# Keys and queries turned on VectorE, and a group's cells sorted by array shape, in an mLSTM and SwiGLU kernel

## The chip, the cores and the metric

The kernel runs on one core of a Trainium2 chip. The metric is the device time of one execution in microseconds. The core has a matrix engine (TensorE, in the profile PE for matmuls and PEld for weight loads), a vector engine (VectorE, DVE), a scalar engine (ScalarE, ACT), a general engine (GpSimd, POOL) and a queue engine (SyncE, SP) that issues all transfers here. Matmuls read SBUF and write PSUM[...]; VectorE and ScalarE read the results from there.

## The reference

Two blocks follow one another. The first is an mLSTM cell over 4 batches, 8 heads, 768 steps, head size 40; the second is a SwiGLU feed-forward over the 3072 tokens of width 320, with an inner width of 1536. All is float32.

```python
def _attn_ref(q, k, v, i_gate, f_gate, o_gate):          # B, H, S, D = 4, 8, 768, 40
    for t in range(S):
        kt, vt, qt = (k[:, :, t], v[:, :, t], q[:, :, t])
        m_new = np.maximum(f_gate[:, :, t] + m, i_gate[:, :, t])
        f_stab = np.exp(f_gate[:, :, t] + m - m_new)
        i_stab = np.exp(i_gate[:, :, t] - m_new)
        m = m_new
        C = f_stab[:, :, None, None] * C + i_stab[:, :, None, None] * np.einsum('bhd,bhe->bhde', vt, kt)
        n = f_stab[:, :, None] * n + i_stab[:, :, None] * kt
        h_tilde = np.einsum('bhde,bhe->bhd', C, qt)
        nq = np.einsum('bhd,bhd->bh', n, qt)[:, :, None]
        denom = np.maximum(np.abs(nq), 1.0)
        o = 1.0 / (1.0 + np.exp(-o_gate[:, :, t]))
        y[:, :, t] = o * h_tilde / denom

def _moe_ref(x, w_gate, w_val, w_out):                   # x: (3072, 320), from y
    g = x @ w_gate
    silu = g * (1.0 / (1.0 + np.exp(-g)))
    val = x @ w_val
    return silu * val @ w_out
```

## The kernel before

The sequence is cut into cells of 128 steps: 6 cells per batch, 24 in all, each with its 8 heads. Three cells form a group, so there are 8 groups, two per batch. Inside a cell the recurrence is written as attention: scores of k against q, weighted by the gates, times v. What came before the cell is carried as a state `C` (with the normaliser as one column more), which is multiplied with q (`qT`, after its product with the decay `e`) and renewed by the product of k with the weighted v (`add`). A group's 384 tokens then go through the feed-forward: 12 hidden blocks and a projection of 36 matmuls.

Each step is a Python generator. A string says in which order the generators are advanced; with that it sets the order on every engine[...]. In `GROUP`, a letter with a number names one step: `H` a hidden block, `J` a third of one 128-token projection, `k` loads of k and q, `v`, `o`, `e`, `w` other loads, `T` the turning of k and q so that the head size lies on the partitions, `S` the scores, `A` the products with v, with the carried state and the renewal of the state, `F` the finishing of a cell (it divides, gates and turns its output), `W` the weights from the gates. While group g is in the feed-forward, the cells of group g+1 are computed and those of g+2 are loaded.

```python
GROUP = """
H0*3 o0*2 e0*2 H1*3 S0*4 G0*2 H2*3 k0*4 v0 H3*3 o1*2 e1*2 H4*3 S1*4 G1*2 H5*3 k1*4 v1 H6*3 o2*2 e2*2 H7*3 S2*4 G2*2
H8*3 k2*4 v2 H9*3 H10*3 w0 w1 H11*3 A0*5 F0*6 w2 J0 T0*4 W0 J1 A1*5 F1*6 W1 J2*3 T1*4 W0*2 J3 A2*5 F2*6 W0 W2 J4 T2*4 W1*2
J5*3 W2*2 W1 J6 W2 J7 J8*3
"""
# START: a longer string for the first two groups, with the gates and the loading of the weights (cut)

    def load_kq(u):
        un = get(u)
        for a, name in ((k, "k"), (q, "q")):
            for two in range(2):
                dst = un[name].rearrange("p (j two) d -> p two j d", two=2)
                nc.sync.dma_start(out=dst[:, two, :, 0:D], in_=tokens(a, u)[:, two * PR:(two + 1) * PR, :])
                yield

    def turn(u, tag):                        # PR = 4 pairs of heads, L = 128
        un = units[u]
        for name, n in (("k", GC), ("q", 2 * GC - 1)):
            tp = psum.tile([128, PR, L], F32, name="tp_kq", tag=tag, bufs=2)
            for j in range(PR):
                nc.tensor.transpose(tp[:, j, :], un[name][:, 2 * j:2 * j + 2, :].rearrange("p h d -> p (h d)"), ident)
            yield
            un[name + "T"] = work.tile([128, PR, L], F32, name=name + "T", bufs=n)
            nc.scalar.copy(un[name + "T"], tp)
            yield

    def attend(u):
        ...
        ys = un["ys"] = [psum.tile([128, PR // 2, L], F32, name="yT", tag="gen") for _ in range(2)]
        ...
        if c > 0:                            # carried state times q: array shape 64*64
            for j in range(PR):
                for two in range(2):
                    r = slice(two * DP, two * DP + DP)
                    onto(two * PR + j, old[r, j, :], un["qT"][r, j, :], False)
            yield
        if c + 1 < NB:                       # renewal of the state: 128*64
            add = psum.tile([128, PR, D1], F32, name="add", tag="cell", bufs=NCELL)
            for h in range(H):
                two, j = divmod(h, PR)
                nc.tensor.matmul(add[two * DP:(two + 1) * DP, j], lhsT=un["k"][:, 2 * j + two, :],
                                 rhs=un["v_w"][:, h, :], start=(j == 0), stop=(j == PR - 1), skip_group_check=True)
            yield
            new = C_ring[u % 2]
            if c > 0:
                d = dec[:, c - 1, b * PR:(b + 1) * PR].unsqueeze(2).to_broadcast([128, PR, D1])
                kept = work.tile([128, PR, D1], F32, name="kept", bufs=1)
                nc.gpsimd.tensor_tensor(kept, old[:, :, 0:D1], d, op=ALU.mult)
                yield
                nc.vector.tensor_tensor(new[:, :, 0:D1], add, kept, op=ALU.add)
            ...
        for h in range(H):                   # weighted scores times v: 128*64
            onto(h, un["v"][:, h, :], un["w"][:, h, :], True)
        yield

    def hidden(g, m, i0=0, i1=GC):
        ...
        ps = [psum.tile([128, TW], F32, name="gv_ps", tag="gen") for _ in range(2)]      # 4 banks in "gen"
        for kc in range(NKC):
            for i in range(2):               # two halves of 64 rows: 64*128
                r = slice(i * HP, (i + 1) * HP)
                nc.tensor.matmul(ps[i][:, cols], lhsT=wgv_sb[r, kc, ts(m, 128)], rhs=xts[g][r, kc, cols], ...)
        yield
        sg = gsp.tile([128, TW], F32, name="sg")
        nc.scalar.activation(sg[:, cols], ps[0][:, cols], AF.Sigmoid if g else AF.Silu)
        yield
        if g:
            nc.vector.tensor_tensor(sg[:, cols], sg[:, cols], ps[0][:, cols], op=ALU.mult)
        nc.vector.tensor_tensor(h_ring[:, (g * NFC + m) % NH, cols], sg[:, cols], ps[1][:, cols], op=ALU.mult)
        yield

    def project(g, i, part):                 # 128*128
        if part == 0:
            hs[g, i] = psum.tile([128, DM], F32, name="o_ps", tag="gen")
        ...                                  # 4 of its 12 matmuls per part; a copy and a store after the last
```

Of the kernel before, what the change touches and what calls it, by code (L numbers as in the profile page):

```python
# [9 lines left out]
F32 = mybir.dt.float32  # L10
# [13 lines left out]
H0*3 o0*2 e0*2 H1*3 S0*4 G0*2 H2*3 k0*4 v0 H3*3 o1*2 e1*2 H4*3 S1*4 G1*2 H5*3 k1*4 v1 H6*3 o2*2 e2*2 H7*3 S2*4 G2*2  # L24
H8*3 k2*4 v2 H9*3 H10*3 w0 w1 H11*3 A0*5 F0*6 w2 J0 T0*4 W0 J1 A1*5 F1*6 W1 J2*3 T1*4 W0*2 J3 A2*5 F2*6 W0 W2 J4 T2*4 W1*2
J5*3 W2*2 W1 J6 W2 J7 J8*3
# [3 lines left out]
pad0 kq1*2 pad0 bar1 v1 pad1 bar2 kq1 pad2 pad4 kq1 pad4 pad5 pad2 which kq0*2 runA v2 pad1 kq0 o2 T1 pad5 T1 tgA  # L30
decA kq0 M1 decA v0 tgA M1 pad3*2 kq2 runB kq2 T1 T0 kq2 W1 M2 T0 T1 o1 W1 M2 kq2 decB o2 decA S1 B decB W1 decB
bar0 W2 B S1 M0 S1 W0 T0 B*2 T0 M0 W0 o0 S0 o0 o1 R0 W0 W2 S0 R0 W2 G2 S0 decA*2 T2 R0 T2*2 G2 T2 R0 E1 S1 S2 C0 R1
R2 R3 C0 G0 R2 S2 G0 R1 G1 S2 C0 R1 C4 R1 A0 C1 store G1 A0*2 F0 v3 A1 R9*2 A1*2 R9 F0 E2 R9 kq3 S2 kq3*2 C1 F0*2
kq3 F0 R2 C1 R2 R8 A1*2 F1 store tgB store H0 kq5 F1 kq5 T3 H0 kq5 tgB A2 kq5 A2 C4 T3 kq8 F1*2 T3 w3 H0 e3 F1 A2
T3 e3 C4 C3 w7 A2*2 C3 e4 decB R3 T5 R3 C2*2 C3 R3 C13 decB H2 C2 R6 F2 C8 R4 H1 R6 W3 F2 H2 T5 H1 S3 R6 W3 R6 H1
H2 R4*2 C13 R4 F2*2 kq4*2 C13 F2 C5 kq4 H3 kq4 C8 R8 W7 R8 W3 C8 C5 H5 o5 H3 o5 W3 R5 S3 C5 C9 R5 H3 R5 T4 C9 R5 H4
H5 T4 R10 H5 o3 C6 o3 C9 C6 H4 R10*2 H6 G5 R8 C6 H4 S3 kq7*2 C7 w4 G5 C7 w5 H9 kq8 S3 G3 v7 H6 G3 v4 C7 o4 R10 H6
C11 e5 T4 C11 H9 A3 T4 A3*2 W4 kq8 H9 H7 C12*2 W4 C11 kq8 W5 A3 R13 C12 A3 R7 W4 S4 H7 F3 R7 W4 H12 R7*2 C14 R11 H7
S4 R14 C14 R11 W5 T5 C14 S4 R11 H8 H12 R16 F3 e5 e4 H12 C17 R11 v6 C17 H13 H8 F3 C10 H8 R12 W5 C17 C10 v5 o4 H11
C10 C18 R15 C18 w6 H13 S4 kq7 v8 T7 C15 C18 H13 H10 w8 C15 H11 T5 C15 H11 C16 R17 C16 R19 A4 H10 T7 kq7 H10 A4*2 F3  # L40
C16 A4*2 C20 F4 S5 kq6 C19 H14 S5 W6 kq6 W7 S5 kq6 S5 C19 kq6 H14 A5*2 C19 C20 W8 J3 W7 H14 R18 C20 F3 J6 C21 F5 W7
W8 C21 W8 J0 C21 F5 C23 J7 G4 C23 J1 W8 C22 C23 C22 W6 J4 F5 C22 J8 W6 G4 F4 F5 J2 F5 J8*2 F4*2 J5 W6 F4 J2*2 J5
T7*2 T8 J5 T8*3 T6*4
# [19 lines left out]
def kernel(  # L63
# [50 lines left out]
    NCONV, NCELL = 2, 2  # L114
    GATED = range(100)
# [37 lines left out]
# [3 lines that stand above are left out]
            for two in range(2):  # L156
                dst = un[name].rearrange("p (j two) d -> p two j d", two=2)
                nc.sync.dma_start(out=dst[:, two, :, 0:D], in_=tokens(a, u)[:, two * PR:(two + 1) * PR, :])  # L158
                yield
# [133 lines left out]
    def pads(r):  # L293
        if r < NRQ:
            nc.vector.memset(q_ring[r][:, :, D:], 0.0)
        nc.vector.memset(k_ring[r][:, :, D:], 0.0)
        yield
        nc.gpsimd.memset(v_ring[r][:, :, D:], 0.0)
        nc.gpsimd.memset(v_ring[r][:, :, D:D1], 1.0)
        if r < NRO:  # L300
            nc.gpsimd.memset(o_ring[r], 0.0)
            nc.gpsimd.memset(lo_ring[r], 0.0)
        if r < 2:
            nc.gpsimd.memset(C_ring[r], 0.0)
        yield
# [79 lines left out]
    C_ring = [const.tile([128, PR, DP], F32, name=f"C{r}") for r in range(2)]  # L385


    state = {}
# [97 lines left out]
    def attend(u):  # L486

        b, c = divmod(u, NB)
        un = units[u]
        old = state.get("C")  # L490
        ys = un["ys"] = [psum.tile([128, PR // 2, L], F32, name="yT", tag="gen") for _ in range(2)]
        fresh = {(two, col) for two in range(2) for col in range(2)}

        def onto(h, lhsT, rhs, last):
            two, col = h // PR, h % 2
            nc.tensor.matmul(ys[two][col * HP:(col + 1) * HP, (h % PR) // 2, :], lhsT=lhsT, rhs=rhs,  # L496
                             start=(two, col) in fresh, stop=last, skip_group_check=True)
            fresh.discard((two, col))

        if c > 0:  # L500
            for j in range(PR):
                for two in range(2):
                    r = slice(two * DP, two * DP + DP)
                    onto(two * PR + j, old[r, j, :], un["qT"][r, j, :], False)
            yield
        if c + 1 < NB:
            add = psum.tile([128, PR, D1], F32, name="add", tag="cell", bufs=NCELL)
            for h in range(H):
                two, j = divmod(h, PR)
                nc.tensor.matmul(add[two * DP:(two + 1) * DP, j], lhsT=un["k"][:, 2 * j + two, :],  # L510
                                 rhs=un["v_w"][:, h, :], start=(j == 0), stop=(j == PR - 1), skip_group_check=True)
            yield
            new = C_ring[u % 2]
            if c > 0:
                d = dec[:, c - 1, b * PR:(b + 1) * PR].unsqueeze(2).to_broadcast([128, PR, D1])
                kept = work.tile([128, PR, D1], F32, name="kept", bufs=1)
                nc.gpsimd.tensor_tensor(kept, old[:, :, 0:D1], d, op=ALU.mult)
                yield
                nc.vector.tensor_tensor(new[:, :, 0:D1], add, kept, op=ALU.add)
            else:  # L520
                nc.vector.tensor_copy(new[:, :, 0:D1], add)
            state["C"] = new
            yield
        for h in range(H):
            onto(h, un["v"][:, h, :], un["w"][:, h, :], True)
        yield
# [61 lines left out]
    def project(g, i, part):  # L588

        if part == 0:  # L590
            hs[g, i] = psum.tile([128, DM], F32, name="o_ps", tag="gen")
# [28 lines left out]
    for u in first + second + third:  # L620
        for name, f in (("kq", load_kq), ("v", load_v), ("W", weigh)):
            stream(f"{name}{u}", f, u)
        stream(f"T{u}", turn, u, "cell")
# [5 lines left out]
    for u in first + second:  # L629
        for name, f in (("o", load_o), ("G", gate_o), ("S", scores), ("A", attend), ("F", finish)):  # L630
            stream(f"{name}{u}", f, u)
    for u in second + third:
        stream(f"w{u}", load_w, u)
# [13 lines left out]

    for g in range(1, NG):
# [5 lines left out]
        for n, u in enumerate(group(g + 1)):  # L654
            for name, f in (("o", load_o), ("G", gate_o), ("e", load_e), ("S", scores), ("A", attend), ("F", finish)):
                stream(f"{name}{n}", f, u)
        for n, u in enumerate(group(g + 2)):
            for name, f in (("k", load_kq), ("v", load_v), ("w", load_w), ("W", weigh)):
                stream(f"{name}{n}", f, u)
            stream(f"T{n}", turn, u, "conv")  # L660
# [31 lines left out]
```

## Time and profile before

| | |
|---|---|
| Times of three runs | 625.66, 628.41, 628.5 us; median 628.41 |
| Profiled run | 624.95 us, span 623.2 us, mean granted TensorE clock 0.994 |
| Hidden matmuls `gv_ps` (L577) | 1980 records, 321.0 us busy |
| Projection `o_ps` (L595) | 576 records, 163.8 us busy |
| Transposes of k and q `tp_kq` (L463) | 192 records, 32.6 us busy |
| Products with v and with the state, `yT` (L496) | 704 records, 44.0 us busy |
| Renewal of the state, `add` (L510) | 320 records, 19.0 us busy |

The profile gives the busy time of each engine, the share of each in 40 equal slices, the chain of work that ended last, and the groups of instructions by line. A form such as 64*128 in a TensorE row is the rows and columns of the array that the instruction uses. Records of matmuls overlap, so the distance between the starts of neighbours says more than their lengths. A list of waits gives, for each pair of instruction and releaser, the sum, the number and the longest of the waits; a timeline gives the start and the length of runs of like instructions.

### The profile page before, as it was taken

Reading aid. Unit: us, or ns where it says so; the run is one execution under the profiler, and the core shown is the slowest. Engines: PE = TensorE matmul, PEld = TensorE weight load, DVE = VectorE, ACT = ScalarE, POOL = GpSimd, SP = SyncE. Lnnn points to the kernel's source line nnn. Section 1 sums busy time; section 2 is a strip of 40 time slices with the busy share of each in tenths; the row PEclk is TensorE's granted clock in tenths of the full one; section 3 lists DMA queues with packets and bytes.
Section 4 is the critical chain, followed back from the end, with each engine's and each line's share of the span. In section 5 each row is a group of like instructions: output and inputs, shape, how many; then the busy total and the mean of one; then the engine's idle time right before and its main releaser. Section 6 shows DMA issues by size and latency. Waiting matters only on the chain.

```text
span 623.2 us, 10981 instructions
## 1 busy us (share of the span) xinstructions
PE 600.9 (96%) x4252; PEld 408.2 (66%) x4252; DVE 286.6 (46%) x630; ACT 243.5 (39%) x514; POOL 174.1 (28%) x250
## 2 busy tenths in 40 slices
PE   7977899999999999999999999999999999999996
PEld 5766766566667666766667666776667666666564
DVE  7278888933445244533445143533445143632320
ACT  3546999962215611182215611182215621111110
POOL 4145756550205211340205221250204221120000
PEclk9998999999999999999999999999999999999999
DMA  9778999219110490107400390107510210000000
GB/s 138 202 97 198 217 214 272 53 48 169 45 35 12 85 182 1 35 22 149 91 35 12 76 188 4 35 17 138 107 34 13 72 32 1 1 22 12 1 3 29
DMA packets 102451, 48.27 MB, mean 77 GB/s; under 512 B 78432, under 2 KB 97216, under 8 KB 102272
## 3 DMA queue, kind: packets, MB, share of 16 engines
q1 hardware_dynamic: 102400, 47.58, 36.3%
q8 instruction: 33, 0.54, 0.4%
q14 instruction: 18, 0.15, 0.1%
HBM read 43.45 MB, written 4.11 MB: 76 GB/s over the span
## 4 chain that ended last, share of the span: by engine, by line
PE 84%; ACT 4%; DMA 4%; DVE 2%; SPq 2%; issue 1%; POOL 1%; ACTq 0%; DVEq 0%; POOLq 0%
PE gv_ps L577 48%; PE o_ps L595 23%; PE yT L496 5%; PE sp L475 3%; PE tp_kq L463 3%; PE add L510 2%; DMA h_ring<-in_moe_w_val_dram 2%; ACT w_sb L449 1%; SPq L158 1%; DMA v<-in_v_dram 1%; ACT low L264 1%; DMA out_dram<-z_sb 1%; ACT L449 1%; DMA w_sb<-M_dram 1%; ACT bits L263 0%
## 5 line engine op out<-in xcount | busy, mean ns | idle before, releaser
L577 PE MATMUL gv_ps<-xT,wgv_sb 64*128 64x384 f32 (+2 forms) x1980 | 321.0, 478 | 10.0 <-POOL wgv_sb L273 6.1
L577 PEld LDWEIGHTS gv_ps<-xT,wgv_sb 64*128 64x128 f32 x1980 | 192.5, 190 | 124.7 <-POOL wgv_sb L273 6.4
L595 PE MATMUL o_ps<-wo_sb,h_ring 128*128 128x320 f32 x576 | 163.8, 437 | 1.3 <-POOL wo_sb L273 0.7
L584 DVE TENSOR_TENSOR sg<-sg,gv_ps 128x384 f32<-128x384 f32 x84 | 46.6, 554 | 217.7 <-ACT sg L581 217.7
L581 ACT ACTIVATE sg<-gv_ps 128x384 f32<-128x384 f32 (+2 forms) x99 | 47.6, 481 | 233.0 <-PE gv_ps L577 232.8
L595 PEld LDWEIGHTS o_ps<-wo_sb,h_ring 128*128 128x128 f32 x576 | 106.3, 190 | 46.5 <-issue 3.6
L549 POOL TENSOR_TENSOR yb<-yb,o 128x512 f32<-128x512 f32 x24 | 30.4, 1269 | 146.7 <-DVE yl L548 146.7
L483 POOL TENSOR_TENSOR qT<-qT,e_bc 128x512 f32<-128x512 f32 x18 | 22.9, 1273 | 134.1 <-ACT sg L581 68.1
L585 DVE TENSOR_TENSOR h_ring<-sg,gv_ps 128x384 f32<-128x384 f32 (+2 forms) x99 | 53.5, 541 | 10.0 <-ACT sg L581 1.3
L449 ACT ACTIVATE w_sb<-w_sb,g_T 128x128 f32<-128x128 f32 x168 | 51.7, 389 | 0.2
L556 ACT COPY yb<-yb 32x512 f32<-32x512 f32 x24 | 14.8, 616 | 86.6 <-POOL yb L549 86.5
L563 DVE STREAM_TRANSPOSE xT<-yb 128x512 f32<-128x512 f32 x24 | 17.0, 710 | 40.1 <-POOL yb L556 39.7
L479 DVE TENSOR_TENSOR w_sb<-sp,w_sb 128x512 f32<-128x512 f32 x48 | 30.9, 682 | 9.7 <-PE sp L475 9.7
L475 PEld LDWEIGHTS sp<-qT,kT 64*128 64x128 f32 x384 | 27.8, 205 | 6.1 <-issue 0.6
L496 PE MATMUL yT<-w_sb,v 128*64 128x128 f32 x384 | 30.7, 284 | 0.0
L475 PE MATMUL sp<-qT,kT 64*128 64x128 f32 x384 | 29.5, 294 | 0.1
L178 POOL COPY lo<-o 32x128 f32<-32x128 f32 x48 | 19.0, 396 | 34.4 <-ACT o L175 30.4
L496 PEld LDWEIGHTS yT<-w_sb,v 128*64 128x64 f32 x384 | 24.8, 140 | 1.6 <-issue 1.6
L273 POOL TENSOR_TENSOR wgv_sb<-low,size 128x512 uint32<-128x512 uint32 (+1 forms) x16 | 19.3, 1205 | 17.8 <-DVE size L269 16.9
L454 POOL TENSOR_TENSOR v_w<-v,w_sb 128x328 f32<-128x328 f32 x20 | 15.0, 750 | 31.5 <-ACT w_sb L449 26.6
L445 POOL TENSOR_SCALAR_AFFINE_SELECT w_sb<-w_sb 128x1024 f32<-128x1024 f32 x21 | 23.0, 1094 | 0.8
L536 DVE STREAM_TRANSPOSE yb<-yT 128x256 f32<-128x256 f32 x48 | 20.2, 439 | 5.3 <-PE yT L496 4.9
(85 smaller groups left out, 464.1 us busy)
## 6 DMA issues: line engine op xcount, KB each, us to landing
w_sb<-M_dram SPq DMA_DIRECT2D x21, 512.0 KB, 5.5
e_bc<-e_dram SPq DMA_DIRECT2D x36, 128.0 KB, 3.6
k<-in_k_dram SPq DMA_DIRECT2D x48, 80.0 KB, 4.0
v<-in_v_dram SPq DMA_DIRECT2D x24, 160.0 KB, 3.7
q<-in_q_dram SPq DMA_DIRECT2D x48, 80.0 KB, 5.0
o<-in_o_gate_dram SPq DMA_DIRECT2D x48, 80.0 KB, 4.1
raw<-in_moe_w_out_dram SPq DMA_DIRECT2D x8, 480.0 KB
out_dram<-z_sb SPq DMA_DIRECT2D x24, 160.0 KB
```

What stands on the lines that cost most here:

```text
L445: nc.gpsimd.affine_select(w, w, compare_op=ALU.is_ge, fill=-NEG, base=0, pattern=[[0, H], [1, L]], channel_multiplier=-1)
L449: nc.scalar.activation(w[:, h], m[h], AF.Exp, bias=g_T[:, c, b * H + h:b * H + h + 1], scale=-1.0)
L475: nc.tensor.matmul(sps[two][:, j, :], lhsT=un["kT"][r, j, :], rhs=un["qT"][r, j, :], start=True, stop=True)
L479: nc.vector.tensor_tensor(w2, un["sp"][two], w2, op=ALU.mult)
L483: (nc.vector if "mb" in un else nc.gpsimd).tensor_tensor(un["qT"], un["qT"], un["e"], op=ALU.mult)
L496: nc.tensor.matmul(ys[two][col * HP:(col + 1) * HP, (h % PR) // 2, :], lhsT=lhsT, rhs=rhs, start=(two, col) in fresh, stop=last, skip_grou ...
L549: (nc.gpsimd if u in GATED else nc.vector).tensor_tensor(yb, yb, un["o"].rearrange("p x (four d) -> p x four d", d=D)[:, :, :, 0:32], op=A ...
L577: nc.tensor.matmul(ps[i][:, cols], lhsT=wgv_sb[r, kc, ts(m, 128)], rhs=xts[g][r, kc, cols], start=(kc == 0), stop=(kc == NKC - 1))
L581: nc.scalar.activation(sg[:, cols], ps[0][:, cols], AF.Sigmoid if g else AF.Silu)
L584: nc.vector.tensor_tensor(sg[:, cols], sg[:, cols], ps[0][:, cols], op=ALU.mult)
L585: nc.vector.tensor_tensor(h_ring[:, (g * NFC + m) % NH, cols], sg[:, cols], ps[1][:, cols], op=ALU.mult)
L595: nc.tensor.matmul(p, lhsT=h_ring[:, (g * NFC + m) % NH, ts(i, 128)], rhs=wo["sb"][:, m, :], start=(m == 0), stop=(m == NFC - 1))
```

## The change

From the fourth group on, k and q no longer come in token by token to be turned by TensorE. They are loaded, for a whole group, in tiles of 32 steps by 32 elements (and 32 by 8 for the rest of the head size) that lie at the place where their turned form belongs, and VectorE transposes each 32x32 block in place of the transposes in PSUM and their copies by ScalarE. k is still loaded in its old form too, for the renewal of the state. The tiles take the space of the buffers through which the weights came in at the start.

`attend` is split in three: `N` renewal of the state, `I` products with v, `P` carried state times q. A group does all renewals and products with v of its three cells, then all products with the state, and then the whole projection. For this there are four states in place of two, and the PSUM tiles of the third cell, of the renewals and of two projections move to other banks. The renewal takes its decay in four vector operations, without the product on GpSimd. The purpose is to take work off TensorE and to let it change its array shape less often.

```diff
 GROUP = """
-H0*3 o0*2 e0*2 H1*3 S0*4 G0*2 H2*3 k0*4 v0 H3*3 o1*2 e1*2 H4*3 S1*4 G1*2 H5*3 k1*4 v1 H6*3 o2*2 e2*2 H7*3 S2*4 G2*2
-H8*3 k2*4 v2 H9*3 H10*3 w0 w1 H11*3 A0*5 F0*6 w2 J0 T0*4 W0 J1 A1*5 F1*6 W1 J2*3 T1*4 W0*2 J3 A2*5 F2*6 W0 W2 J4 T2*4 W1*2
-J5*3 W2*2 W1 J6 W2 J7 J8*3
+H0*3 o0*2 e0*2 x0*2 H1*3 x0*6 S0*4 G0*2 o1*2 e1*2 H2*3 x1*8 H3*3 k0*2 v0 S1*4 G1*2 H4*3 o2*2 e2*2 x2*8 H5*3 x3*4 H6*3 S2*4
+G2*2 x3*4 H7*3 k1*2 v1 T0*4 H8*3 k2*2 v2 T1*4 w0 w1 H9*3 H10*3 W0 H11*3 W1 N0*2 N1*2 I0 N2*2 I1 I2 w2 W0*2 P0 P1 P2 F0*2 J0
+W1*2 F1*2 W0 J1 F0*3 F2 J2*3 F1*3 F2*4 W2*2 J3 W2 W1 T2*4 J4 J5*3 W2 J6 J7 J8*3
 """
 ...                                  (START: each A becomes its N, I and P at nearly the same place)
+    def place_x():
+        for n in range(4):
+            x = conv.tile([128, 2 * NPW], U32, name="raw", bufs=NRAW).bitcast(F32)[:, 0:2 * GC * L]
+            xs.append(x.rearrange("p (j n e) -> p j n e", j=2, e=32))
+            nc.vector.memset(xs[n][:, :, :, LO:], 0.0)
+
+    def load_x(g, n):
+        b, c = divmod(g * GC, NB)
+        a, h0 = (k, q)[n // 2], n % 2 * 2
+        for two in range(2):
+            for p, d0, d1 in ((0, 0, 32), (32, 32, D)):
+                p += two * DP
+                for j in range(2):
+                    src = a[b, two * PR + h0 + j, ds(c * L, TW), d0:d1].rearrange("(n s) d -> s n d", s=32)
+                    nc.sync.dma_start(out=xs[n][p:p + 32, j, :, 0:d1 - d0], in_=src)
+                    yield
+
+    def load_k(u):                    (the k half of load_kq)
+
+    def turn_x(u):
+        sq = slice(u % GC * NSQ, u % GC * NSQ + NSQ)
+        for i, (name, n) in enumerate((("k", GC), ("q", 2 * GC - 1))):
+            t = get(u)[name + "T"] = work.tile([128, PR, L], F32, name=name + "T", bufs=n)
+            for m in range(2):
+                nc.vector.transpose(t[:, 2 * m:2 * m + 2, :].rearrange("p j (n e) -> p j n e", e=32), xs[2 * i + m][:, :, sq])
+                yield
 ...
-    C_ring = [const.tile([128, PR, DP], F32, name=f"C{r}") for r in range(2)]
+    C_ring = [const.tile([128, PR, DP], F32, name=f"C{r}") for r in range(GC + 1)]
 ...
-    def attend(u):
+    def within(u, tag, last):         (I)
+        for h in range(H):
+            onto(u, tag, h, units[u]["v"][:, h, :], units[u]["w"][:, h, :], last)
+        yield
+
+    def before(u, tag, last):         (P)
+        if u % NB > 0:
+            old = C_ring[(u - 1) % (GC + 1)]
+            for j in range(PR):
+                for two in range(2):
+                    r = slice(two * DP, two * DP + DP)
+                    onto(u, tag, two * PR + j, old[r, j, :], units[u]["qT"][r, j, :], last)
+            yield
+
+    def newer(u, tag):                (N: the add matmuls as before)
+            old, new = (C_ring[x % (GC + 1)] for x in (u - 1, u))
             if c > 0:
-                d = dec[:, c - 1, b * PR:(b + 1) * PR].unsqueeze(2).to_broadcast([128, PR, D1])
-                kept = work.tile([128, PR, D1], F32, name="kept", bufs=1)
-                nc.gpsimd.tensor_tensor(kept, old[:, :, 0:D1], d, op=ALU.mult)
-                yield
-                nc.vector.tensor_tensor(new[:, :, 0:D1], add, kept, op=ALU.add)
+                for j in range(PR):
+                    nc.vector.scalar_tensor_tensor(new[:, j, 0:D1], in0=old[:, j, 0:D1],
+                                                   scalar=dec[:, c - 1, b * PR + j:b * PR + j + 1], in1=add[:, j],
+                                                   op0=ALU.mult, op1=ALU.add)
 ...
     def project(g, i, part):
         if part == 0:
-            hs[g, i] = psum.tile([128, DM], F32, name="o_ps", tag="gen")
+            tag = "conv" if g and i < 2 else "gen"
+            hs[g, i] = psum.tile([128, DM], F32, name="o_ps", tag=tag, bufs=PB[tag])
 ...
     for g in range(1, NG):
 ...
+            tag = "gen" if n < 2 else "cell"
+            stream(f"N{n}", newer, u, "conv")
+            stream(f"I{n}", within, u, tag, u % NB == 0)
+            stream(f"P{n}", before, u, tag, True)
 ...
+        if g + 2 < NG:
+            for n in range(4):
+                stream(f"x{n}", load_x, g + 2, n)
```

## The prediction

> **What bounds the kernel now.** I read the page first: the busy times, then the 40 slices, then the chain of work that ended last.
>
> ```profile
> span 623.2 us, 10981 instructions
> ...
> PE 600.9 (96%) x4252; PEld 408.2 (66%) x4252; DVE 286.6 (46%) x630; ACT 243.5 (39%) x514; POOL 174.1 (28%) x250
> ...
> PE   7977899999999999999999999999999999999996
> ...
> PE 84%; ACT 4%; DMA 4%; DVE 2%; SPq 2%; issue 1%; POOL 1%; ACTq 0%; DVEq 0%; POOLq 0%
> PE gv_ps L577 48%; PE o_ps L595 23%; PE yT L496 5%; PE sp L475 3%; PE tp_kq L463 3%; PE add L510 2%; DMA h_ring<-in_moe_w_val_dram 2%; ACT w_sb L449 1%; SPq L158 1%; DMA v<-in_v_dram 1%; ACT low L264 1%; DMA out_dram<-z_sb 1%; ACT L449 1%; DMA w_sb<-M_dram 1%; ACT bits L263 0%
> ```
>
> TensorE is busy 96% of the span and is 84% of the chain; from the sixth slice on (about 78 us) every slice but the last shows 90% or more. Nothing else is above half. So from the first group loop on, every microsecond of TensorE issue removed is one off the time, as long as no other engine makes it wait. The list of waits, kept to TensorE, agrees: its longest entries all belong to the start.
>
> ```profile
> PE gv_ps L577 <- POOL wgv_sb L273: 6.1, 2, 3.1
> PE gv_ps L577 <- DVE xT L563: 3.5, 1, 3.5
> ```
>
> A busy engine may still lose time between its pieces. For that I looked at one group in the timeline of TensorE (start, length, line, operation, count; an fp32 matmul leaves two records, so x8 is four matmuls):
>
> ```profile
> 321.35 0.74 PE L510 MATMUL add<-v_w,k 128*64 128x41 f32 x13
> ...
> 322.09 1.07 PE L496 MATMUL yT<-w_sb,v 128*64 128x128 f32 x14
> 323.09 2.42 PE L595 MATMUL o_ps<-wo_sb,h_ring 128*128 128x320 f32 x8
> 325.35 0.60 PE L463 MATMUL tp_kq<-ident,k 128*128 128x128 f32 x4
> 325.79 0.60 PE L463 MATMUL tp_kq<-ident,q 128*128 128x128 f32 x4
> 326.22 2.32 PE L595 MATMUL o_ps<-wo_sb,h_ring 128*128 128x320 f32 x8
> 328.47 0.67 PE L496 MATMUL yT<-qT,C 64*64 64x128 f32 x16
> 329.07 0.74 PE L510 MATMUL add<-v_w,k 128*64 128x41 f32 x13
> ```
>
> Take starts, not lengths, since matmuls overlap. The two transposes hold TensorE from 325.35 to 326.22, 0.87 us per cell. And each row's array shape (128*64, 128*128, 64*64) differs from its neighbour's: one cell goes through three shapes and is cut off from the next by a piece of projection. The groups after the start repeat every 70.5 to 70.6 us: the first hidden block after a projection starts at 209.28, 279.77 and 350.37.
>
> [...] Single projection records start 269 ns apart. From the last one to the first 64*64 record the distance is 362 ns (+93); the first 64*64 round of four then takes 140 ns in place of 109 (+31). From the last yT record of a cell to the projection it is 203 in place of 109 ns (+94), and the first projection record takes 373 in place of 269 (+104). From projection to the 128*128 transposes it is 269: no charge without a change of shape. [...]the old k and q packets are already 160 B, and take 19 ns on average in the trace.
>
> **The change, part by part.**
>
> 1. Transposes off TensorE. The start still transposes on TensorE for the cells of the first three groups. The last five groups, 15 cells, lose 0.87 us each: 13.1 us. The ScalarE copies out of PSUM (0.59 us each, two per cell) go too, on an engine with slack.
>
> 2. Fewer changes of shape. From the distances above a change costs: into projection 0.20, from projection into 64*64 0.12, from 64*64 into 128*64 0.12 (200 in place of 89 ns, then 79 in place of 58), projection into hidden 0.20 (362 for 269, then 420 for 316), hidden into 128*64 0.12. Before, a group whose first cell opens a sequence pays hidden-to-cell 0.12, then 0.20, then twice 0.44, then 0.20: 1.41 us. A group with carried state in all three cells pays three times 0.44 and 0.20: 1.53 us. After, all 128*64 work comes first, then the 64*64 products, then all 36 projection matmuls: 0.12 + 0.12 + 0.20 + 0.20 = 0.65 us in both. Saved 0.76 and 0.88; the six groups with cells are three of each: 4.9 us.
>
> 3. New on VectorE: per cell four 32x32-block transposes of 128x256. The same shape out of PSUM took 0.44 us (yb, 48 of them), so 1.8 us per cell. They follow the vector work of hidden blocks 7 and 8, the third cell's follow the finishing work. A hidden block lasts 3.23 us on TensorE and needs 1.2 us of VectorE,
>
> ```profile
> 245.03 0.56 DVE L584 TENSOR_TENSOR sg<-sg,gv_ps 128x384 f32<-128x384 f32 x1 [2.01 <-ACT sg L581]
> 245.69 0.55 DVE L585 TENSOR_TENSOR h_ring<-sg,gv_ps 128x384 f32<-128x384 f32 x1
> ```
>
> with 2.01 us idle before it. 1.8 fits in 2.0, so this is hidden if the tiles have landed. Each state update becomes four vector operations (estimate 0.2 us each, from the 0.19 us of the small den operation) for one of 0.32, and its GpSimd product of 0.46 us goes; in a group this is hidden, because three yT products (0.87 us each) stand between the updates and their readers.
>
> 4. New on the DMA queue: 32 loads per group for k and q in place of the 6 for q alone; k is still loaded in its old form for the state update. In the old trace two loads of one kind cost the queue 1.05 to 1.14 us:
>
> ```profile
> 213.97 1.05 SPq L158 DMA_DIRECT2D q<-in_q_dram  x2
> 215.07 0.51 SPq L162 DMA_DIRECT2D v<-in_v_dram  x1
> 215.68 1.02 SPq L170 DMA_DIRECT2D o<-in_o_gate_dram  x2
> 216.75 1.09 SPq L403 DMA_DIRECT2D e_bc<-e_dram  x2
> ```
>
> that is about 0.58 us each with the gaps. Before the first vector transpose stand 32 tile loads and 13 to 15 others: 47 x 0.58 = 27.3 us, and the queue begins 1.2 us after the group does, so the last tile load is issued about 28.5 us into the group and lands some 4 us later (k took 4.0, q 5.0): 32 to 33 us. Packets: 32 x 384 = 12288 small ones; at 14 to 19 ns over 16 engines 11 to 15 us, inside those 27.
>
> When is it needed? Block 7 ends at 8 x 3.23 + 3 x 0.89 + 0.1 = 28.6 us, its vector work 1.85 later (as 250.86 to 252.69 for the last block), 30.4; two k transposes and one q bring 31.8. VectorE may be held there a while: TensorE waits only if block 8's vector work is not done when block 10 needs its PSUM pair, at 35.1 us. Back from there (1.2 for the vector work, 0.5 for the last transpose): the tiles may land as late as 33.3. So it is hidden by about a microsecond, or just not. I charge 0.5 us per group on average, 2.5 us.
>
> 5. The start. Its order is nearly the same, but VectorE is 70 to 90% busy in most slices there; four carried updates cost it 0.5 us more each, and there are some more fills. I charge 0.5 us.
>
> Sum: -13.1 - 4.9 + 2.5 + 0.5 = -15.0 us. The three times were 625.66, 628.41 and 628.5, and the profiled run 624.95; the middle of these is about 627, which gives 612. The update products now follow each other and can share the two column halves better (a cell's products took 0.73 us for 0.46 us of one half's work); for this I take 1 us more: 611.0 us.
>
> **The rivals.**
>
> Rival A, the loads come late. VectorE would stop in front of the first transposes, and with it the hidden blocks behind. For: 32 to 33 us against 33.3 is no margin, and around 213 to 232 the 16 DMA engines are already saturated, with queue instructions held up to 1.80 us. Against: packets that small take 14 ns when undisturbed. If the loads land 4 us later than I think, five groups lose up to 4 us each: 628, no gain at all. If the tile packets cost twice the old ones, 25 us of DMA, it is about 2 us each: 618.
>
> Rival B, the finishing of the cells is squeezed. The 64*64 products now end only about 6 us after the last hidden block, and the three cells' finishing (VectorE about 4 us each, with 2.1 us for GpSimd and ScalarE between) must fit in the 19.4 us of projection, 72 records of 269 ns. My count ends 5 to 6 us before the next group. If the exponentials queued ahead on ScalarE (two times 2.4 us and a table load of 1.28) wait for late w loads, this is used up: up to 3 us for each of six groups, 625 at worst.
>
> Rival C, [...]then only the transposes count, 627 - 13.1 + 3 = 617.
>
> **Range and chances.** Without any new wait: 627 - 18 = 609, less a microsecond or two for the packing: 607. With the DMA late by 2 us per group: about 619. So 605 to 619 should hold it 8 times in 10. The 2% limit is 615.8; A, or B and C together, would pass it: faster 0.80, same 0.18, slower 0.02.
>
> **What would show it.** Group distance of 67.1 us in place of 70.6 in the timeline of TensorE; one unbroken projection of 72 records, 19.4 us; four changes of shape per group; no transposes after 140 us. TensorE's busy time would fall by about 18 us and its idle time stay near 22. Wrong would be: hidden matmuls that wait for h_ring or sg behind vector transposes which wait for the raw tiles (A), or a first hidden block that waits for xT (B).

## The result and the profile after

The changed kernel takes 605.48 us (median of four runs, 604.90 to 605.88), where the kernel before took 627.03 us (median of four, 625.27 to 628.50). The ratio is 0.9657, with a 95% interval of 0.9623 to 0.9691. The prediction was 611 us, 605 to 619: right, near the favourable end.

The page of the profile after, from the busy times to the chain of work that ended last:

```profile
span 603.9 us, 11003 instructions
...
PE 580.7 (96%) x4132; PEld 393.9 (65%) x4132; DVE 316.0 (52%) x742; ACT 227.8 (38%) x484; POOL 167.2 (28%) x236
...
PE   7877899999999999999999999999999999999996
...
PEclk9878799999999999999999999999999999999999
...
PE 85%; DVE 5%; DMA 3%; ACT 2%; POOL 2%; issue 1%; SPq 1%; DVEq 0%; ACTq 0%; POOLq 0%
```

TensorE still sets the time: it is busy for 96% of a shorter span. It has 120 records fewer, which are the 15 cells' eight transpose records each. VectorE has taken over 29 us, and its share rises to 52%, with idle time left. The span is 19.3 us shorter and TensorE's busy time 20.2 us.

The timeline of TensorE shows one whole group of the changed kernel (columns: start, length, engine, line, operation, operands, records). L605 is the hidden block, L543 the renewal, L517 the products with v and with the state, L624 the projection:

```profile
206.07 6.72 PE L605 MATMUL gv_ps<-xT,wgv_sb 64*128 64x384 f32 x40
...
247.65 1.26 PE L543 MATMUL add<-v_w,k 128*64 128x41 f32 x29
...
248.92 2.81 PE L517 MATMUL yT<-w_sb,v 128*64 128x128 f32 x46
251.66 1.54 PE L517 MATMUL yT<-qT,C 64*64 64x128 f32 x48
253.13 19.65 PE L624 MATMUL o_ps<-wo_sb,h_ring 128*128 128x320 f32 x72
272.71 6.72 PE L605 MATMUL gv_ps<-xT,wgv_sb 64*128 64x384 f32 x40
```

All 128*64 work stands in one run, all 64*64 work in the next, and the 72 projection records are unbroken. From 206.07 to 272.71 are 66.64 us, where the group of this kind took 70.49 before. Such distances between the first hidden blocks of neighbouring groups come out the same to 0.03 us in the four traces that share the groups' code (the changed kernel twice, e6 and e11 below), so they are what the experiments are read by. I call a group **opening** when its first cell begins a sequence (the others **carried**).

The list of waits of TensorE is as telling for what it lacks. Its longest entries are (columns: who waited for whom, us in total, times, longest in us):

```profile
PE gv_ps L605 <- DVE xT L591: 3.5, 1, 3.5
PE gv_ps L605 <- DVE C L549: 3.0, 1, 3.0
PE gv_ps L605 <- POOL wgv_sb L297: 2.8, 1, 2.8
```

Each occurs once and in the start (62, 43 and 54 us). Nothing in the groups waits for the vector transposes or for the tiles.

### The profile page after: what moved, and what is told of

It reads as the page before. It is cut to its first block, busy times and chain, and to the rows that moved or that the text cites. A ratio compares the mean times of both kernels' runs of the same rounds, so it can differ in the third digit from the quotient of the medians.

```text
span 603.9 us, 11003 instructions
## 1 busy us (share of the span) xinstructions
PE 580.7 (96%) x4132; PEld 393.9 (65%) x4132; DVE 316.0 (52%) x742; ACT 227.8 (38%) x484; POOL 167.2 (28%) x236
## 4 chain that ended last, share of the span: by engine, by line
PE 85%; DVE 5%; DMA 3%; ACT 2%; POOL 2%; issue 1%; SPq 1%; DVEq 0%; ACTq 0%; POOLq 0%
PE gv_ps L605 48%; PE o_ps L624 23%; PE yT L517 5%; PE sp L498 3%; PE add L543 2%; PE mb L443 2%; PE tp_kq L486 1%; DMA raw<-in_moe_w_out_dram 1%; POOL wo_sb L297 1%; DMA e_bc<-e_dram 1%; DMA v<-in_v_dram 1%; ACT w_sb L472 1%; DMA out_dram<-z_sb 1%; DVE size L293 0%; DVE bits L292 0%
## 5 line engine op out<-in xcount | busy, mean ns | idle before, releaser
L605 PE MATMUL gv_ps<-xT,wgv_sb 64*128 64x384 f32 (+2 forms) x1980 | 323.5, 480 | 9.7 <-DVE xT L591 3.5
L605 PEld LDWEIGHTS gv_ps<-xT,wgv_sb 64*128 64x128 f32 x1980 | 193.2, 192 | 126.2 <-POOL wgv_sb L297 6.4
L624 PE MATMUL o_ps<-wo_sb,h_ring 128*128 128x320 f32 x576 | 158.0, 434 | 0.9 <-POOL wo_sb L297 0.7
L624 PEld LDWEIGHTS o_ps<-wo_sb,h_ring 128*128 128x128 f32 x576 | 108.5, 190 | 48.1 <-POOL wo_sb L297 1.8
L584 ACT COPY yb<-yb 32x512 f32<-32x512 f32 x24 | 14.8, 616 | 60.3 <-POOL yb L577 60.0
L629 ACT COPY z_sb<-o_ps 128x320 f32<-128x320 f32 x24 | 10.1, 421 | 48.2 <-issue 25.3
L517 PE MATMUL yT<-w_sb,v 128*64 128x128 f32 x384 | 27.5, 282 | 0.0
L517 PEld LDWEIGHTS yT<-w_sb,v 128*64 128x64 f32 x384 | 23.8, 141 | 1.1 <-issue 1.1
L564 DVE STREAM_TRANSPOSE yb<-yT 128x256 f32<-128x256 f32 x48 | 18.8, 427 | 7.4 <-PE yT L517 7.4
```

The costliest lines, as they stand in the source:

```text
L517: nc.tensor.matmul(un["ys"][two][col * HP:(col + 1) * HP, (h % PR) // 2, :], lhsT=lhsT, rhs=rhs, start=(two, col) in un["fresh"], stop=las ...
L624: nc.tensor.matmul(p, lhsT=h_ring[:, (g * NFC + m) % NH, ts(i, 128)], rhs=wo["sb"][:, m, :], start=(m == 0), stop=(m == NFC - 1))
```

## The experiments

All are edits of the changed kernel. Times are medians of all runs with their range. Groups and start are read from the one profiled run, which need not lie at the median (e2's took 616.41 us). The last column is where the first hidden block of the second group starts, which is the length of the start.

| kernel | us | opening group | carried group | start |
|---|---|---|---|---|
| before (profiled run: 624.95) | 627.03 (625.27-628.50) | 70.61 | 70.49 | 138.67 |
| changed | 605.48 (604.90-605.88) | 66.95 | 66.64 | 139.13 |
| changed, again | 605.52 (602.98-605.88) | 66.95 | 66.64 | 139.21 |
| e1_pe_turn | 655.95 (654.44-660.82) | 75.6-75.9 | 77.5-77.6 | 141.85 |
| e7_pe_turn_placed | 619.86 (618.23-622.88) | 69.57-69.63 | 69.27 | 141.82 |
| e2_cell_by_cell | 612.29 (611.83-616.41) | 67.98 | 67.86 | 143.15 |
| e3_state_between | 610.60 (609.45-614.21) | 67.51 | 67.36 | 141.02 |
| e4_add_alternate | 605.24 (603.63-608.63) | 66.69-66.73 | 66.33 | 138.75 |
| e8_alternate_n2_later | 605.29 (604.68-607.05) | 66.36 | 66.33 | 140.83 |
| e5_turn_early | 616.76 (615.32-619.99) | 66.9-71.2 | 69.2-69.8 | 141.04 |
| e6_renew_as_before | 608.15 (606.84-609.19) | 66.95 | 66.64 | 140.62 |
| e9_with_start_renewal | 603.84 (601.69-606.10) | 66.36 | 66.33 | 137.96 |
| e11_changed_filled | 598.35 (597.68-599.18) | 66.94 | 66.64 | 131.91 |
| e10_filled_start | 598.08 (596.87-599.47) | 66.36 | 66.33 | 133.37 |

**What are the transposes worth by themselves?** The order of the cells stays sorted, but k and q are loaded as before and turned by TensorE.

```diff
-            for name, f in (("k", load_k), ("v", load_v), ("w", load_w), ("T", turn_x), ("W", weigh)):
+            for name, f in (("k", load_kq), ("v", load_v), ("w", load_w), ("W", weigh)):
+            stream(f"T{n}", turn, u, "cell")
-... J3 W2 W1 T2*4 J4 J5*3 W2 J6 J7 J8*3
+... W2*2 J3 W2 W1 J4 T0*4 J5*3 T1*4 W2 J6 T2*4 J7 J8*3
```

> The changed kernel with its cells sorted by shape, but k and q of the later groups loaded in the old form and turned by TensorE at the end of the projection, where the shape is 128*128 already. Theory (every transpose is TensorE issue time, shape changes are apart from it): 15 cells x 0.87 us come back, so about 605.5 + 13.1 = 618.6 us, and the groups are 69.3 to 69.6 us apart in place of 66.6 to 66.9. Rival (the gain comes from the sorting, the transposes were mostly filling): under 611 us.

It took 655.95 us, worse than either kernel, and fits neither theory. The waits of TensorE in this run say why:

```profile
PE tp_kq L486 <- ACT kT L489: 24.8, 5, 5.7
```

The first cell's copies out of PSUM stood on ScalarE behind the third cell's finishing and behind eight exponentials, which waited for GpSimd (5.2 and 1.2 us in the first of these groups). GpSimd's own work for the exponentials began within 0.1 us of what stood ahead of it there, so it was the order on the engines that held the copies, and not a late load, as I thought when I wrote the next expectation. TensorE needed those PSUM buffers for the next cell and stood still for 4.4 to 5.7 us in each of five groups; with each stop its granted clock fell to half for 3.4 or 6.8 us (the four transpose records behind the first stop took 1.12 us, where they took 0.60 ahead of it). This run measures my placing, not the transposes. So I placed them again, one cell at a time between pieces of projection, with the copies ahead of those exponentials. The transposes now use the PSUM buffers that two projections had, so all projections go back to their old ones:

```diff
+F0*2 J0 W1*2 F1*2 W0 J1 F0*3 T0*4 F2 J2*3 F1*3 J3 T1*4 F2*4 J4 J5*3 T2*4 W2*2 W2 W1 J6 W2 J7 J8*3
+            stream(f"T{n}", turn, u, "conv")
```

> The changed kernel, sorted by shape, with k and q of the later groups loaded in the old form and turned by TensorE, this time one cell at a time between pieces of the projection, with the ScalarE copies placed ahead of work that waits for late loads (in the first try TensorE waited 24.8 us for these copies). Theory: groups 0.87 x 3 = 2.62 us longer than the changed kernel's 66.64 and 66.94, so 69.26 and 69.56, five groups, +13.1 us, about 619 us. Rival (TensorE transposes between projections are cheaper than their records say): groups less than 1.5 us longer.

Groups with transposes are 2.63 us longer than in the changed kernel (69.57 and 69.27), the last one, which has none, is 66.64 as there: 2.63 x 5 = 13.1 us. The trace of the kernel before had it already: its sixth group, which turns no cells, took 67.86 us where the others of its kind took 70.49. TensorE's timeline shows the cost directly:

```profile
263.73 4.47 PE L624 MATMUL o_ps<-wo_sb,h_ring 128*128 128x320 f32 x16
268.04 0.60 PE L486 MATMUL tp_kq<-ident,k 128*128 128x128 f32 x4
268.48 0.60 PE L486 MATMUL tp_kq<-ident,q 128*128 128x128 f32 x4
268.92 4.47 PE L624 MATMUL o_ps<-wo_sb,h_ring 128*128 128x320 f32 x16
```

From 268.04 to 268.92 are 0.88 us, three times in the group: no shape changes here, so the transposes cost their issue time and nothing more. The rival is out.

**What is the sorting worth?** First the vector transposes alone, with the cells worked off one by one:

```diff
-W0 H11*3 W1 N0*2 N1*2 I0 N2*2 I1 I2 w2 W0*2 P0 P1 P2 F0*2 J0 W1*2 F1*2 W0 J1 ...
+H11*3 N0*2 I0 P0 F0*5 w2 J0 W0 J1 N1*2 I1 P1 F1*5 W1 J2*3 W0*2 J3 N2*2 I2 P2 F2*5 ...
-            tag = "conv" if g and i < 2 else "gen"
+            tag = "gen"
```

> The changed kernel with its vector transposes, but the cells worked off one by one with pieces of projection between them, as before. Theory[...]: 0.76 and 0.88 us per group for the shapes and about 0.3 us for the renewal products that no longer follow each other, six groups: +6.7 us, about 612.2 us. Rival (changes of shape cost nothing, the whole gain is the transposes): within 2 us of 605.5.

Groups are 1.03 and 1.22 us longer, 6.8 us over six groups; the median is 612.29, 6.8 above 605.5. The expectation was met. At 67.98 and 67.86 us they are also the groups of the kernel before less the 2.63 us of the transposes, so in the groups the new loads, the vector transposes and the four-part renewal add nothing on balance. This run mixes two effects: more changes of shape, and renewals that no longer follow each other. The next one changes the number of shapes only:

```diff
-P0 P1 P2 F0*2 J0
-W1*2 F1*2 W0 J1 F0*3 F2 J2*3
+P0 F0*2 J0
+P1 W1*2 F1*2 W0 J1 P2 F0*3 F2 J2*3
```

> The changed kernel, but the products with the carried state stand one before each third of the projection; the renewals and the products with v stay sorted. This adds only changes between 128*128 and 64*64 and back: two pairs in a group with carried state in three cells, one pair in the other kind. Theory: 0.32 us a pair (0.12 out, 0.20 back), so +0.64 us and +0.32 us per group, +2.9 us in all, about 608.4 us. Rival (the gain of sorting is in the packing of the renewals, not in the shapes): within 1 us of 605.5.

In the carried group the products with the state now stand between pieces of projection:

```profile
254.10 0.67 PE L517 MATMUL yT<-qT,C 64*64 64x128 f32 x16
254.70 2.42 PE L624 MATMUL o_ps<-wo_sb,h_ring 128*128 128x320 f32 x8
257.05 0.67 PE L517 MATMUL yT<-qT,C 64*64 64x128 f32 x16
...
260.60 15.34 PE L624 MATMUL o_ps<-wo_sb,h_ring 128*128 128x320 f32 x56
```

Carried groups are 0.72 us longer: 0.36 us for each of the two added pairs, where 0.32 was expected. Opening groups are 0.56 us longer where I had expected 0.32; there I had miscounted. With the first third of the projection ahead of both products, that group also gains a change from the products with v to the projection (0.20) and two pairs (0.64), less the change it no longer makes (0.12) and the one return it had already (0.20): 0.52. So 3.8 us in the groups, with the same matmuls in number and kind. The rival is out: these shape changes cost time, 0.36 us a pair. The median, 610.60, is 5.1 us up. The two profiled runs are 5.7 apart: 3.8 in the groups, and 1.9 in the start, which the edit does not touch (see below).

**Where does the rest of the sorting's gain come from?** Per group 0.3 us came beyond the shapes. In the changed kernel the first renewal does four heads in one column half of the array, then four in the other. In its trace the run of renewals that begins at 247.65 us has its first five starts one by one, 58 to 79 ns apart; only from 247.91, 0.26 us in, do other starts fall between them. I read this as one half without work for 0.26 us, and let the heads alternate:

```diff
             for h in range(H):
-                two, j = divmod(h, PR)
+                j, two = divmod(h, 2)
+                h = two * PR + j
```

> The changed kernel, with the eight matmuls of a renewal alternating between the two column halves of the array, where they did four in one half and then four in the other. Theory ([...]a half idles while the other does its first four): 0.26 us less for every run of renewals, one or two runs per group: -2.3 us over six groups, about 603 us; the first 16 records then start in pairs. Rival (weight loads of the two halves don't overlap, or the half idle at the start is made up at the end): no difference.

Records now start in pairs, 6 ns apart and a pair every 58 ns, and a carried group is 0.31 us shorter. The median, 605.24, does not show it, as the runs spread over 5 us. An opening group has two runs of renewals, but gained only 0.23 to 0.25. The timeline of this run shows a gap in front of the third renewal:

```profile
181.29 1.07 PE L517 MATMUL yT<-w_sb,v 128*64 128x128 f32 x16
182.47 0.67 PE L544 MATMUL add<-v_w,k 128*64 128x41 f32 x16
182.95 1.95 PE L517 MATMUL yT<-w_sb,v 128*64 128x128 f32 x32
```

From 181.29 to 182.47 are 1.18 us for work that takes 0.87. The renewals rotate through two PSUM buffers, and the third one needs the buffer of the first, which VectorE was reading until 182.41; 0.05 us later it starts. Putting it behind the second product with v should free it of that:

```diff
-N0*2 N1*2 I0 N2*2 I1 I2
+N0*2 N1*2 I0 I1 N2*2 I2
```

> The renewals alternating between the column halves, and the third renewal moved behind the second product with v, since in the run before it started 378 ns after its neighbour, waiting for its PSUM bank. Theory (a wait took the place of the gain there): groups with three renewals 66.94 - 2 x 0.26 = 66.4 us apart in place of 66.7, the others stay at 66.3; about 2.5 us below the changed kernel in all. Rival (the gap belongs to something else, such as the change from 128 to 41 columns): 66.7 us as before.

Opening groups come to 66.36 us, as expected: 0.59 below the changed kernel, twice the 0.3 of a single run of renewals. In the timeline of this run, the 32 records of the two products now lead straight into the renewal, 1.78 us later (32 records at 109 ns a pair are 1.74):

```profile
183.36 1.95 PE L517 MATMUL yT<-w_sb,v 128*64 128x128 f32 x32
185.14 0.61 PE L544 MATMUL add<-v_w,k 128*64 128x41 f32 x16
```

The groups together give 2.7 us. The median, 605.29, does not show them: the start of the profiled run was 1.7 us longer.

**How near were the tiles to being late?** The loads stay, the vector transposes of two cells go two hidden blocks ahead:

```diff
-G2*2 x3*4 H7*3 k1*2 v1 T0*4 H8*3 k2*2 v2 T1*4
+x3*8 H5*3 T0*4 H6*3 T1*4 S2*4 G2*2 H7*3 k1*2 v1 H8*3 k2*2 v2
```

> The changed kernel, with the vector transposes of the first two cells put after hidden blocks 5 and 6 in place of 7 and 8; the loads stay where they are. Theory (the last tiles land some 28 to 29 us into a group, 1.6 us before VectorE asks for them and 4 to 5 us before TensorE would feel it): VectorE now waits for the tiles at about 24 us, hidden blocks wait behind it, 1 to 3 us in four of the five groups, +4 to +11 us in all. Rival (the tiles land far ahead of their use): within 1 us of 605.5, with no wait of the transposes for raw.

VectorE now stands in front of the q tiles, with the next hidden block's work behind it:

```profile
232.83 0.45 DVE L182 STREAM_TRANSPOSE qT<-raw 128x256 f32<-128x256 f32 x1 [1.00 <-DMA raw<-in_q_dram]
237.02 0.45 DVE L182 STREAM_TRANSPOSE qT<-raw 128x256 f32<-128x256 f32 x1 [3.75 <-DMA raw<-in_q_dram]
237.39 0.52 DVE L612 TENSOR_TENSOR sg<-sg,gv_ps 128x384 f32<-128x384 f32 x1
```

That group began at 207.98, so the last tile was usable 29.0 us into it. Four of the five groups were 2.5 to 4.2 us longer, 12.4 us in all, and the median 11.3 us higher: a little over the upper end of the expectation. In the longest of them TensorE also ran at half clock for 3.4 us after its stop of 1.96 us: the 80 hidden records behind the stop took 15.37 us, where they took 14.22 in the other three, so 1.15 of its 4.2 us. The first of the five groups did not lose; its last tile came 24.6 us into it in the changed kernel, and 28.5 us in the next. The theory holds: the loads are hidden because VectorE asks for q only 31.2 us into the group (237.24 in the group from 206.07), not because they are far ahead.

**The start.** The four vector operations of the renewal were suspected there, as the wait of 3.0 us for C named them.

```diff
-                for j in range(PR):
-                    nc.vector.scalar_tensor_tensor(new[:, j, 0:D1], in0=old[:, j, 0:D1], ...)
+                nc.gpsimd.tensor_tensor(kept, old[:, :, 0:D1], d, op=ALU.mult)
+                nc.vector.tensor_tensor(new[:, :, 0:D1], add, kept, op=ALU.add)
```

> The changed kernel with the renewal of the state as before: decay product on GpSimd and one addition on VectorE in place of four vector operations. Theory (only the start feels it, where a hidden matmul waited 3.0 us for the state on VectorE): groups 66.6 to 66.9 us apart as in the changed kernel, the first block of the second group at 138.7 in place of 139.1, so -0.5 us. Rival (the four operations are part of the gain): the time rises by 1 us or more, with products that wait for C in the groups.

Groups are the same to the hundredth, so there the four operations neither help nor cost. The expected 0.5 us off the start did not come: it was longer, 140.62, and the median higher, 608.15. By then starts between 138.7 and 143.2 us stood beside one another, several of the very same code. So I ran the changed kernel again, and beside it the start's old renewal in the best version:

```diff
+                if u < 2 * GC:        # the cells of the start
+                    nc.gpsimd.tensor_tensor(kept, old[:, :, 0:D1], d, op=ALU.mult)
+                    nc.vector.tensor_tensor(new[:, :, 0:D1], add, kept, op=ALU.add)
+                else:                 # as changed
```

> The changed kernel once more, on the same chip as these. Theory (the groups are fixed, the start varies with the granted clock): groups 66.94 and 66.64 us apart to 0.05 us; the first block of the second group may lie anywhere from 138.5 to 143 us, as it did in the kernels with the same start. Rival (the start of 139.1 us belongs to this kernel): 139.1 us again to 0.3 us.

> As the run with alternating renewals and the third one later, and in the start alone the renewal as it was before the change (product on GpSimd, one addition on VectorE). Theory (the four vector operations cost the start about 1.2 us, where VectorE is busy, and nothing in the groups): 1 us below that run, the first hidden matmul no longer waits for C. Rival (what the start takes is set by when the clock is granted): within 0.5 us on the median, with the first block of the second group anywhere between 138.5 and 143 us.

The changed kernel repeated its groups and, by chance, its start (139.21 for 139.13); but it got there in another way. The same work of the two runs, first the changed kernel's first profile, then its second:

```profile
18.72 1.04 PE L433 MATMUL mb<-late,ident_b 128*128 128x512 bf16 x2
19.69 1.28 PE L443 MATMUL mb<-f_sb,ident 32*128 32x128 f32 x8
```

```profile
18.75 1.04 PE L433 MATMUL mb<-late,ident_b 128*128 128x512 bf16 x2
19.72 2.07 PE L443 MATMUL mb<-f_sb,ident 32*128 32x128 f32 x8
```

The same eight records take 1.28 and 2.07 us. The clock records of the two traces agree: full rate was first granted at 20.0 us in the one and at 39.6 us in the other. The first lost its lead again to half-rate stretches up to 67.8 us, the second had its last one before 60.1. Where the start's code and the clock record are both the same, so is the start: e3 and e5 were first granted the full rate at 51.6 us and started their second group at 141.02 and 141.04; e1 and e7 were granted it at 39.8 and started at 141.85 and 141.82.

The second run also answers for the renewal, since e6 has nearly its clock record (39.8 us, held from 60.3). The block that was said to wait for C waits as long without the four operations:

```profile
45.94 2.07 PE L605 MATMUL gv_ps<-xT,wgv_sb 64*128 64x128 f32 x20 [2.97 <-DVE C L549]
```

```profile
45.98 1.92 PE L605 MATMUL gv_ps<-xT,wgv_sb 64*128 64x128 f32 x20 [2.97 <-POOL wgv_sb L297]
...
53.91 0.42 PE L376 MATMUL dec_ps<-dec_r,halves 32*128 32x48 f32 x2 [1.39 <-DVE C L551]
```

In the changed kernel C and the weights were ready within 0.1 us of each other (45.90 and 45.88), and the list of waits named the later one. In e6 (second fence) C was ready only at 46.71, and the block did not wait for it. Its old product stands on GpSimd behind the preparation of weights, so the next C comes late too, at 53.85, and TensorE waits 1.39 us for that. With like clocks the old renewal makes the start 1.4 us longer (140.62 for 139.21), so by these two traces the four operations help there. e9 came to 603.84 us, 1.5 below e8, but its profile has an early grant (20.4 us), so this gain isn't shown to be the renewal's.

The half clock costs the start time (2.07 us for 1.28 above). That it would come less if TensorE's gaps were filled was a guess of mine, which none of these traces had shown. To try it, matmuls whose results nobody reads were put into gaps of the start; the output is the same, and the work is more:

```diff
+        for _ in range(8 if u == 2 else 0):
+            nc.tensor.matmul(units[u]["mb"][0], lhsT=ident_b, rhs=late..., start=True, stop=True, ...)   # bf16 128x512
+        for _ in range({(0, 0): 8, (1, 0): 8, (2, 0): 8, (0, 1): 12}.get((m, i0), 0) if g == 0 and i1 - i0 < GC else 0):
+            nc.tensor.matmul(ps[0], lhsT=ident_b, rhs=late..., start=True, stop=True)                   # bf16 128x384
```

> The changed kernel with matmuls that nobody reads in the start: eight of bf16 128x512 behind the first products, and 8 to 12 of bf16 128x384 ahead of the first three hidden blocks that wait for their weights and ahead of the one that waits for xT. They fill gaps in which TensorE was idle, and compute nothing. Theory (the start's spread of 138.7 to 143.2 us is the half clock[...]): the clock is granted earlier and kept, the start ends at 133 to 138 us, groups stay at 66.64 and 66.94. Rival (the start is bound by loads and by VectorE, the clock only moves where TensorE waits): 139 to 141 us as before, and the median within 1 us of 605.5.

> The same filling in the best version so far (renewals alternating, third renewal later, the start's renewals as before the change). Theory: 2 to 5 us below its 603.8 us, and the runs closer together than its 601.7 to 606.1. Rival: within 1 us of 603.8.

Both took 598 us, 7 us below the changed kernel. In e11 the start ended at 131.91 us, ahead of the whole range expected; e10 came 5.8 us below e9, also more than expected, and its runs lie closer together (2.6 us apart, 4.4 in e9). TensorE's timeline of e11:

```profile
2.82 3.62 PE L433 MATMUL mb<-late,ident_b 128*128 128x512 bf16 x8
...
7.46 2.03 PE L446 MATMUL mb<-f_sb,ident 32*128 32x128 f32 x16
```

The 16 records that took 3.78 us before (and in the changed kernel) take 2.03. The clock was granted at 6.3 us, as expected, but against the expectation it was not kept: half rate came back from 20.0 to 33.6 us. e10 adds the shorter groups, 2.7 us, and is not faster than e11: its start is 1.5 us longer (133.37). Both starts still depend on when the half clock comes, so whether the alternating renewals cost anything there is left open. Against the kernel before, e11 stands at 0.9548 (0.9514 to 0.9582) and e10 at 0.9548 (0.9508 to 0.9587): the best versions, level with each other.

## Why the prediction was right

Point by point, with the terms of its sum:

- **Transposes, -13.1 us: right.** e7 gives 2.63 us per group, 13.1 over five.
- **Changes of shape, -4.9 us: right as far as tested.** e2 gives 6.8 us in the groups for shapes and packing together; e3 gives 0.36 us for a pair whose worth was put at 0.32. The other changes of shape were not tried one by one.
- **Packing of the renewals, -1.0 us: too small.** Groups became 3.66 (opening) and 3.85 us (carried) shorter; after 2.62 for transposes and 0.76 or 0.88 for shapes, 0.28 and 0.35 us are left, 1.9 us over six groups. e4 supports the mechanism: where four heads of one column half come first, starts in pairs begin 0.26 us late, and to alternate them won 0.31 us for one run. Sorting saves one such run per group. Alternating them in the unsorted order was not tried.
- **Late tiles, +2.5 us: not paid.** Here lay the largest error in size. The mechanism, a wait of VectorE for the tiles that reaches TensorE only through the hidden blocks, is what e5 shows; but I had put the last landing at 32 to 33 us, and it was 28.5. In their long rows the tile loads took the queue 0.52 us each and not 0.58; all 47 loads took 26.1 us in place of 27.3:

```profile
225.10 8.26 SPq L168 DMA_DIRECT2D raw<-in_q_dram  x16
```

  And they landed about a microsecond after their issue had ended, where I had taken 4. The tile packets needed 8.6 us of 16 engines per group and not 11 to 15: in the trace 13.5 ns for 128 B and 8.7 ns for 32 B. The transposes themselves took 0.40 us each, 0.44 estimated. The changed kernel's VectorE did not wait:

```profile
236.50 0.78 DVE L182 STREAM_TRANSPOSE kT<-raw 128x256 f32<-128x256 f32 x2
237.24 0.84 DVE L182 STREAM_TRANSPOSE qT<-raw 128x256 f32<-128x256 f32 x2
238.60 0.56 DVE L612 TENSOR_TENSOR sg<-sg,gv_ps 128x384 f32<-128x384 f32 x1 [0.52 <-ACT sg L609]
```

  The idle 2.01 us in front of the block's work has become 0.52: the new work fits into the old gap.
- **The start, +0.5 us: right in size by luck.** It is 0.46 us longer in the profiled pair, whose clocks differ. Against the second run of the changed kernel it is 0.54 us, but there the first grant came 1.2 us later than before (39.6 for 38.4), which at half rate can be worth 0.6 us, an estimate from these two records. The reason given, four vector operations for each carried update, is contradicted by e6.

Rival A (late loads) didn't happen; e5 shows what it costs when VectorE asks too early. Rival B (squeezed finishing) didn't happen: in the group from 206.07 the last xT was written at 269.4 us, 3.3 us before the next hidden block. That margin is smaller than the 5 to 6 us I had counted. Rival C (the transposes alone count) is ruled out by e3, with its 0.36 us a pair.

The sum, -13.1 - 4.9 - 1.9 + 0.5 = -19.4, matches the difference of the two profiled spans, 19.3. It is 3.4 us more than predicted, 2.5 of it for the tiles and 0.9 for the packing. As the packing is what the groups leave over, this says that nothing was gained or lost outside the groups and the start; how the groups' 6.8 us divide between shapes and packing rests on e3 and e4. The medians differ by 21.5 us. Nearly all of the other 2 us is the spread of the kernel before: its profiled run was at the lower end, while two of its four runs took 628.4 and 628.5. This spread goes with the clock: the mean granted clock of every run is on record (it leaves out the time ahead of the first grant), and among 38 runs of the kernel before that stand beside the experiments, the twelve at 0.994 took 624.9 to 625.7 us, the seven at 0.978 625.6 to 625.9 and the four at 0.987 628.5 to 628.6. Only one of the 38, at 0.989, stands more than 1 us apart from the others of its clock.

## What to carry to other kernels

When one engine is busy from end to end, take its work by issue time, from start to start of neighbouring records, and not by the lengths of overlapping ones: such sums held here to a tenth of a microsecond per group. Put work of one array shape together (a pair of changes took 0.36 us in e3), and let neighbours in order use different parts of the array (0.31 us for a run of renewals in e4); then look for the wait that takes the place of what was saved (e4's second run of renewals gave its gain back to a PSUM buffer still unread). A transpose moved to an engine with idle gaps was free here because its loads landed before that engine's turn; two hidden blocks earlier in the order it cost 12 us (e5). And when a list of waits names a cause, take that cause away before believing it: the wait for C stayed 2.97 us without it.

## What the runs showed of the hardware that was not expected

In the second run of the changed kernel TensorE had next to no gap from 7.4 to 26.8 us, with float32 matmuls on 32 rows of the array, float32 transposes and scores, and yet the full rate was first granted at 39.6 us; the scores at the end of that stretch, 16 records, took 2.08 us, where the first run, granted at 20.0 us, took 1.16 for the same. So being busy for these 19.4 us was not enough. With eight more bf16 matmuls on all 128 rows, the grant came at 6.3 us (e11, where their records took 3.62 us) and at 5.2 us (e10, 3.06 us), where none of the twelve traces without filling had it before 19.8 us; with the later fillings the start became 7.2 us shorter. Whether the rows, the type or the length of these matmuls counts was not separated. Three of those twelve traces had the grant near 20 us, with nearly the same instructions up to there; what decides it between runs was not tried. In the groups the clock fell to half with each of the five stops of TensorE in e1, 4.4 to 5.7 us long, and with one of 1.96 us in e5, but not with the stops of 1.2, 1.4 and 1.8 us in e5: after those the next 80 records took 14.22 us each time, and 15.37 after the one of 1.96. Whether the length of a stop alone decides this was not tried.
